# A linear-attention and expert-attention kernel: one drawn-up order for all instructions, fixed buffers, and scores on row halves

## The chip, the cores and the metric

The kernel runs on one core of one Trainium2 chip. A core has TensorE (PE) for matrix products, with PSUM banks as its output; VectorE (DVE), ScalarE (ACT) and GpSimd (POOL) for elementwise work; SyncE (SP) and the other engines' queues issue the transfers (DMAs) between HBM and SBUF. The metric is device time in microseconds (us). Before the change the median of three runs is 376.76 us (375.64 to 377.31).

## The reference, cut to what matters

A gated linear attention makes x, and a small mixture of four attention experts with a top-2 gate works on x. All of it is float32.

```python
# q, k, v, alpha: (4, 8, 768, 48); alpha in 0.8 to 1
for t in range(S):
    state = alpha[:, :, t, :, None] * state + einsum('bhd,bhe->bhde', k[:, :, t], v[:, :, t])
    y[:, :, t] = einsum('bhd,bhde->bhe', q[:, :, t], state)
x = y.transpose(0, 2, 1, 3).reshape(4, 768, 384)
logits = x @ w_gate                              # (384, 4): the two largest of 4, softmax over them
for e in range(4):
    q, k, v = x @ wq[e], x @ wk[e], x @ wv[e]    # (384, 64) each
    scores = where(causal, -1e9, scale * (q @ k.T))
    a = softmax(scores)
    ye = a @ v @ wo[e]                           # (64, 384)
    out += (e is one of the two) * gate_weight * ye
```

## The kernel before, in words

**Tiles.** The 768 positions of each of four batches are cut into six chunks of 128, so there are 24 chunks. Three chunks are one unit of the expert attention: eight units, u = 0 to 7, of 384 positions. Heads come in pairs, one on partitions 0 to 47 and one on 64 to 111.

**Linear attention, per chunk.** Three loads bring decay factors (al, line 85), queries with keys (qk, line 94) and values (v, line 100). DVE scans the decay factors backwards (line 187, into r) and forwards (line 197, into c), takes reciprocals (line 190), and multiplies keys by r (line 199) and queries by c (line 200). PE makes the products pa of keys and queries, two row halves of 48 rows, 8 matmuls of 128 columns into two PSUM banks, named pa. Each of the two banks is masked: the first by a DVE product (line 219); the second for chunks 0 to 2 also by DVE, and for later chunks by an ACT copy (line 221) and a POOL select (line 222). Four transposes (pt) and eight small matmuls (pu) update the state: DVE adds (line 256), POOL multiplies (line 257), or DVE alone (line 254) in a batch's first chunk. PE forms py, x of the chunk; ACT copies it to a rounded high half xh (line 283), and DVE subtracts to get a low half xl (line 284). ACT sums the squares of al (line 204) for a check on its range.

**Expert attention, per unit.** The front of a unit is four projections pj (9 matmuls of 384 columns each: high times high, high times low, low times high), three value projections pv, and the gate on DVE. The back is twelve score tiles (two pairs of experts, two experts, three groups of 128 rows), their softmax and the rest. Before, a score uses fp32r operands: queries and keys as high and low halves, stacked over 128 partitions, so that two matmuls over 128 rows make one tile. The high halves are ACT copies (lines 411, 434), the low halves are DVE subtractions (lines 412, 435, 430, 431), and transfers on SP from SBUF to SBUF (lines 418 and 438) put the halves on the partitions where they are wanted. DVE adds the causal mask, writes the tile and finds the row minimum of its negative (line 503); ACT takes the exponential (line 506), DVE the reciprocals of the sums (lines 514, 515), POOL multiplies with these and the gate (line 520). PE transposes (line 537, tr), ACT copies (line 548), PE multiplies by the values (yv) and, with a high and a low half again (lines 568, 569), by wo (po). ACT copies to ot (line 580), SP stores (line 583).

**What sets the order.** The function `head()` (lines 306 to 346) lists the work of the first three chunks by hand, in `tc.manual_schedule()`. Behind it `mix()` (line 633) draws from streams: a unit's back, the next unit's front, and the chunks of the unit after that (`gla()`, line 367). Each stream has a weight (`MIX_BACK`, `MIX_FRONT`, `MIX_GLA`), and the stream that has had the least matmul cost by its weight goes next. Tiles come from pools whose buffers rotate: eight PSUM banks for all products, 3 buffers for al and v, 4 for qk, 7 for score tiles a. `gla()` issues its loads on ACT's queue, the head on SP's. Matmuls on zeros (`warm()`, 56 in all) stand between the head's steps. At the very end (lines 657 to 664) DVE counts the chunks whose squares are in range, a matmul with ones sums the count (line 660, pk), a cast stores it (line 662), and a branch on the value picks a slow repetition of everything if it falls short.

## Time and profile before

| | before |
|---|---|
| median of 3 runs | 376.76 us (375.64 to 377.31) |
| the profiled execution | 377.36 us |
| its span in the trace | 375.6 us |
| mean granted clock of PE | 0.967 |
| PE busy | 339.1 us, 90% of the span |
| DVE busy | 256.6 us, 68% |
| ACT busy | 215.5 us, 57% |
| POOL busy | 117.6 us, 31% |
| HBM read and written | 24.44 and 4.72 MB, 78 GB/s over the span |

The span is the time from the first to the last event in the trace of the profiled execution; its own time is 1.76 us longer. An engine's busy time is the time in which it executes something; register, branch, semaphore and issuing instructions are not counted. The granted clock is a share of TensorE's full clock, 2.4 GHz. A high busy share over the whole run says little about one stage of it, so the rows further down also cut the run into stretches.

### The profile page before, as it was taken

The numbers are of one execution on the slowest core, as the hardware profiler recorded it, in microseconds if no ns is written. First come the engines' busy times: TensorE is split into PE (matmuls) and PEld (weight loads), VectorE is DVE, ScalarE is ACT, GpSimd is POOL, SyncE is SP. The second block draws the span as 40 slices with busy tenths as digits, with TensorE's granted clock in tenths as the row PEclk, the third lists the DMA queues.
The fourth block names the chain that finished last, engine by engine and source line by source line (L and its number), as shares of the span: only waits on it lengthen the run. The fifth ranks groups of instructions, "written<-read, shape, count | busy, mean of one in ns | idle before, by whom it ended". The sixth has DMA issues, their size and how long they took to land.

```text
span 375.6 us, 9749 instructions
## 1 busy us (share of the span) xinstructions
PE 339.1 (90%) x3654; PEld 283.9 (76%) x3654; DVE 256.6 (68%) x729; ACT 215.5 (57%) x540; POOL 117.6 (31%) x192
## 2 busy tenths in 40 slices
PE   7879829889976999899899999999999999999993
PEld 5568717678955977687779888787889977988772
DVE  5999998687777979367857889175538641576610
ACT  1246555644434978275546896375548853868740
POOL 2040139402123750034403751043305620425500
PEclk9899965999998999999999999999999999999997
DMA  7764671368477334564376525463264005541101
GB/s 241 282 205 120 126 179 26 103 206 217 126 179 186 121 101 115 156 171 115 98 172 176 145 92 142 128 157 88 66 162 119 4 7 156 144 111 50 42 23 52
DMA packets 23400, 47.97 MB, mean 128 GB/s; under 512 B 3536, under 2 KB 10416, under 8 KB 23344
## 3 DMA queue, kind: packets, MB, share of 16 engines
q1 hardware_dynamic: 15744, 29.39, 29.3%
q10 hardware_dynamic: 7600, 17.87, 17.0%
q8 instruction: 31, 0.51, 0.6%
q14 instruction: 25, 0.20, 0.2%
HBM read 24.44 MB, written 4.72 MB: 78 GB/s over the span
## 4 chain that ended last, share of the span: by engine, by line
PE 62%; DVE 15%; DMA 9%; ACT 7%; issue 4%; POOL 2%; ACTq 0%; DVEq 0%; POOLq 0%; SPq 0%
PE pj L72 10%; PE yv L72 10%; PE sc L72 8%; PE tr L537 8%; PE py L72 7%; PE po L72 7%; PE pv L72 5%; DMA al<-in_al_dram 5%; PE pa L72 3%; DVE al L187 3%; DMA qk<-in_qk_dram 2%; DVE al L197 2%; ACT al L204 2%; DMA q<-tq 2%; PE pu L72 2%
## 5 line engine op out<-in xcount | busy, mean ns | idle before, releaser
L520 POOL TENSOR_SCALAR a<-a,sc,gw 128x128 f32<-128x128 f32 (+5 forms) x96 | 76.2, 804 | 84.2 <-DVE sc L515 52.1
L506 ACT ACTIVATE a<-a,mx 128x512 f32<-128x512 f32 (+5 forms) x96 | 63.7, 665 | 33.7 <-DVE mx L503 33.1
L72 PE MATMUL sc<-k,q 128*128 128x384 f32 (+3 forms) x256 | 59.2, 348 | 6.5 <-DVE xl L284 3.2
L503 DVE CUSTOM_DVE_ANT_0 a<-sc,cm 128x384 f32<-128x384 f32 (+3 forms) x96 | 49.3, 528 | 17.4 <-PE sc L72 15.1
L537 PE MATMUL tr<-ident,a 128*128 128x128 f32 x336 | 50.5, 280 | 7.6 <-POOL a L520 7.6
L548 ACT ACTIVATE at<-tr 128x512 f32<-128x512 f32 (+3 forms) x124 | 49.6, 460 | 4.3 <-PE tr L537 3.9
L72 PEld LDWEIGHTS sc<-k,q 128*128 128x128 f32 x256 | 42.2, 196 | 11.4 <-DVE xl L284 3.5
L72 PE MATMUL yv<-at,vg 128*64 128x384 f32 (+2 forms) x324 | 47.0, 394 | 2.9 <-ACT at L548 2.9
L537 PEld LDWEIGHTS tr<-ident,a 128*128 128x128 f32 x336 | 39.2, 143 | 13.3 <-POOL a L520 9.9
L72 PEld LDWEIGHTS yv<-at,vg 128*64 128x64 f32 x324 | 24.5, 136 | 23.4 <-issue 12.7
L72 PE MATMUL py<-ms,v 128*32 128x128 f32 x768 | 36.7, 285 | 3.1 <-DVE ms L219 1.6
L187 DVE TENSOR_TENSOR_SCAN al<-al,d1r 112x516 f32<-112x516 f32 (+1 forms) x25 | 29.6, 1184 | 13.9 <-DMA al<-in_al_dram 13.9
L72 PE MATMUL pj<-xl,wqk_h 128*128 128x384 f32 x96 | 33.2, 346 | 2.2 <-DVE xl L284 2.2
L72 PE MATMUL pj<-xh,wqk_h 128*128 128x384 f32 x96 | 34.5, 361 | 0.8 <-ACT xh L283 0.6
L257 POOL TENSOR_TENSOR S<-st,ev 48x192 f32<-48x192 f32 x32 | 16.9, 528 | 56.2 <-DVE st L256 55.2
L191 POOL COPY ev<-al 112x4 f32<-112x4 f32 (+1 forms) x25 | 6.4, 256 | 87.5 <-DVE S L254 51.0
L72 PE MATMUL pj<-xh,wqk_l 128*128 128x384 f32 x96 | 33.0, 344 | 0.0
L204 ACT ACTIVATE al<-al 112x1033 f32<-112x1033 f32 x23 | 24.6, 1069 | 14.1 <-POOL ev L191 5.4
L197 DVE TENSOR_TENSOR_SCAN al<-al,d1c 112x516 f32<-112x516 f32 (+1 forms) x25 | 30.6, 1223 | 0.5
L72 PE MATMUL pa<-qk 48*128 48x128 f32 x384 | 28.2, 285 | 2.4 <-issue 1.5
L72 PEld LDWEIGHTS py<-ms,v 128*32 128x32 f32 x768 | 23.0, 113 | 9.2 <-DVE ms L219 3.0
L72 PEld LDWEIGHTS pa<-qk 48*128 48x128 f32 x384 | 23.4, 187 | 4.8 <-issue 2.0
(98 smaller groups left out, 645.3 us busy)
## 6 DMA issues: line engine op xcount, KB each, us to landing
q<-tq SPq DMA_DIRECT2D x64, 192.0 KB, 3.6
qk<-in_qk_dram ACTq DMA_DIRECT2D x18, 448.0 KB, 4.6
k<-tk SPq DMA_DIRECT2D x56, 96.0 KB, 3.1
v<-in_v_dram ACTq DMA_DIRECT2D x19, 256.0 KB, 3.9
out_dram<-ot SPq DMA_DIRECT2D x24, 192.0 KB, 1.9
al<-in_al_dram ACTq DMA_DIRECT2D x18, 226.2 KB, 2.9
qk<-in_qk_dram SPq DMA_DIRECT2D x5, 448.0 KB, 5.9
v<-in_v_dram SPq DMA_DIRECT2D x5, 256.0 KB, 6.1
```

Source lines behind the costliest of these rows:

```text
L72: return PE.matmul(out, lhsT, rhs, **kw)
L187: V.tensor_tensor_scan(backwards(al[0:P, AW + c0 - 1:AW + c1 - 1]), backwards(al[0:P, c0:c1]), d1r[0:P, sl].rearrange("p a w -> p (a w)"), ...
L191: G.tensor_copy(gl["ev", n][0:P, sl], r[:, :, 0])
L197: V.tensor_tensor_scan(c.rearrange("p a w -> p (a w)"), c.rearrange("p a w -> p (a w)"), d1[0:P, sl].rearrange("p a w -> p (a w)"), 0.0, O ...
L204: A.activation(al, al, AF.Square, accum_out=acc[0:P, n:n + 1])
L257: G.tensor_tensor(Ln[rows, :, cols], st[rows], e, OP.mult)
L503: V.tensor_tensor_reduce(a[:, c0:c1], pp[:, :w], cm[:, m0:m0 + w], -1.0, mx[:, 0:1] if x else BIG, OP.add, OP.min, accum_out=mx[:, x:x + 1])
L506: A.activation(a[:, 0:n], a[:, 0:n], AF.Exp, bias=nm, scale=-1.0, accum_out=sm)
L520: G.tensor_scalar(a[:, 0:n], a[:, 0:n], cf[:, x:x + 1], mo["w", u][:, i, eg:eg + 1], op0=OP.mult, op1=OP.mult)
L537: PE.transpose(pt[:, 128 * (j - j0):128 * (j - j0) + 128], a[:, 128 * j:128 * j + 128], ident)
L548: A.activation(dst, src, AF.Copy)
```

## The change

**A plan in place of pools and streams.** A class `Plan` takes each piece of work as a record: engine, the time for which it occupies the engine, the time until its result is there, what it reads and writes, and a function that issues it. `schedule()` walks through time: of the records on each engine whose inputs are there and whose buffers are free it takes the one that can start first (within `LOOK` = 0.05 us the earlier record in the source), and allots one of a fixed number of buffers. The durations are numbers in the source, as `vec`, `act`, `pol` and constants for PE. `emit()` issues all records in that order in `tc.manual_schedule()`, and puts matmuls on zeros into PE's gaps of over 0.45 us before 45 us of the plan's time, 88 in all. The streams and `mix()` still set the order of the records in the source.

**Buffers.** Seven PSUM banks for products, and one for the matmuls on zeros; 4 buffers for al, qk, values and ev, 8 score tiles, 4 for at, 2 for ms.

**Scores.** Queries and keys are ACT copies in f32, one tile per pair of experts, with one expert on partitions 0 to 63 and the other on 64 to 127. A score is one f32 matmul over 64 rows for each expert, the two side by side on row halves. The low halves of queries and keys and the transfers from SBUF to SBUF are gone. Score matmuls go from 256 to 128. Scores are made per pair of experts, `AHEAD` is 3 pairs in place of 5 tiles.

**Other edits.** All loads go through SP. The second mask goes to ACT and POOL for all chunks (`MS_DVE = 0`). The check at the end stands behind the last po.

**How the orders differ.** On DVE, at the head, the instructions up to the one that subtracts chunk 2's low half (xl) in the order before. In it al and qk are decay factors and queries with keys, d1c holds reciprocals, ms is a mask's result, S and st are states, and a scan is named SCALAR_TENSOR_TENSOR on al:

```order
L187 SCALAR_TENSOR_TENSOR al<-al,d1r 112x516
L190 RECIPROCAL d1c_80<-al 112x4
L199 TENSOR_TENSOR qk<-qk,al 112x4x128
L219 TENSOR_TENSOR ms<-pa_343,mask 128x512
L219 TENSOR_TENSOR ms<-pa_344,mask 128x512
L197 SCALAR_TENSOR_TENSOR al<-al,d1c_80 112x516
L172 SCALAR_TENSOR_TENSOR wqk_l<-wqk,wqk_h 128x3x256
L176 TENSOR_TENSOR wqk_l<-wqk,wqk_h 128x3x256
L200 TENSOR_TENSOR qk<-qk,al 112x4x128
L284 TENSOR_TENSOR xl<-py,xh 128x3x128
```

The same place on DVE in the new order, where g_63 to g_69 are the seven PSUM banks, at_137 holds the raw weights and al_73 and qk_77 belong to chunk 3:

```order
L454 TENSOR_TENSOR ms_90<-g_67,mask 128x512
L393 SCALAR_TENSOR_TENSOR al_73<-al_73,d1r 112x516
L397 RECIPROCAL d1c_87<-al_73 112x4
L508 TENSOR_TENSOR st_93<-g_63,S_95 48x192
L338 SCALAR_TENSOR_TENSOR wqk_l<-at_137,wqk_h 128x3x256
L342 TENSOR_TENSOR wqk_l<-at_137,wqk_h 128x3x256
L548 TENSOR_TENSOR xl_98<-g_69,xh_96 128x3x128
L508 TENSOR_TENSOR st_93<-g_63,S_95 48x192
L416 SCALAR_TENSOR_TENSOR al_73<-al_73,d1c_87 112x516
L420 TENSOR_TENSOR qk_77<-qk_77,al_73 112x4x128
```

Chunk 3's second scan and its products moved from ahead of chunk 2's low half to behind it, and one of chunk 2's two masks left DVE.

On PE, scores of the second unit in the order before, with transposes (tr) of other tiles between them; k_579 and k_580 are the keys of the two experts of a pair, x2 stands for the high and the low queries:

```order
L72 MATMUL sc<-k_579,q 128x512 x2
L72 MATMUL sc<-k_579,q 128x256 x2
L537 MATMUL tr<-ident,a 128x128 x4
L72 MATMUL sc<-k_580,q 128x512 x2
L537 MATMUL tr<-ident,a 128x128 x5
```

The corresponding place on PE in the new order, where k_105 and q_103 hold two experts each and line 698 is the transposes:

```order
L642 MATMUL g_66<-k_105,q_103 128x512
L642 MATMUL g_68<-k_105,q_103 128x512
L698 MATMUL g_65<-ident,a_133 128x128 x4
L698 MATMUL g_63<-ident,a_134 128x128 x4
L642 MATMUL g_69<-k_105,q_103 128x256
L642 MATMUL g_67<-k_105,q_103 128x256
L642 MATMUL g_64<-k_105,q_103 128x384
L642 MATMUL g_65<-k_105,q_103 128x384
```

Two consecutive matmuls of one tile became two consecutive matmuls of two tiles, one for each expert, which hold two banks at once.

On SP, the queue in the order before, from the last loads of the head on; tq and tk are the halves that transfers from SBUF to SBUF put in place, ot is an output tile:

```order
L100 DMA v<-in_v_dram 128x512
L94 DMA qk<-in_qk_dram 112x1024
L85 DMA al<-in_al_dram 112x517
L418 DMA q<-tq 64x768 x8
L583 DMA out_dram<-ot 128x384 x3
L418 DMA q<-tq 64x768 x4
L438 DMA k_448<-tk 64x384 x2
L438 DMA k_449<-tk 64x384 x2
```

SP's queue in the new order, at the first stores; al_72, qk_77 and vt_81 are buffers of decay factors, queries with keys, and values:

```order
L311 DMA qk_77<-in_qk_dram 112x1024
L316 DMA vt_81<-in_v_dram 128x512
L307 DMA al_72<-in_al_dram 112x517
L767 DMA out_dram<-ot_145 128x384
L767 DMA out_dram<-ot_146 128x384
L307 DMA al_73<-in_al_dram 112x517
L767 DMA out_dram<-ot_145 128x384
L311 DMA qk_74<-in_qk_dram 112x1024
L316 DMA vt_78<-in_v_dram 128x512
```

The loads of all later chunks came into SP's queue, between stores, and the transfers of queries and keys left it.

The core of the diff:

```diff
-AB = 7
-XB = 2
...
+AHEAD = 3
+HOP = 0.1
...
+ISSUE = 3.0
+SEM = 0.07
+DMA_FIXED = 1.5
+DMA_RATE = 220.0
+LOOK = 0.05
+WARM_UNTIL = 45.0
+WARM_GAP = 0.45
+WARM_MM = 0.11
+GB = 7
+MS_DVE = 0
+class Plan:
...
+    def schedule(self, timed=True):
+        ops, pools = self.ops, self.pools
+        slot_of, done = {}, [None] * len(ops)
+        free = {p: [(0.0, x) for x in range(len(t))] for p, t in pools.items()}
...
+            if timed:
+                for e, lst in ready.items():
+                    c = [(est(i), i) for i in lst]
+                    c = [x for x in c if x[0] is not None]
+                    if not c:
+                        continue
+                    lo = min(x[0] for x in c)
+                    t, i = min((x for x in c if x[0] <= lo + LOOK), key=lambda x: x[1])
+                    if best is None or t < best[0]:
+                        best = (t, i)
...
+            o["start"] = t
+            at[e] = t + o["occ"]
+            end = t + o["lat"]
+            if o["dma"]:
+                dma_at = max(t + DMA_FIXED, dma_at) + o["dma"] / DMA_RATE / 1e3
+                end = dma_at
+            o["end"] = end
...
+            for j in succ[i]:
+                same = ops[j]["eng"] == e and not o["dma"]
+                rt[j] = max(rt[j], t + o["occ"] if same else end + SEM)
...
+    def emit(self, warm=None):
+        pe = ISSUE
+        for i in self.order:
+            o = self.ops[i]
+            if warm is not None and o["eng"] == "PE":
+                gap = o["start"] - pe
+                if o["start"] < WARM_UNTIL and gap > WARM_GAP:
+                    warm(int(gap / WARM_MM * 0.8))
+                pe = o["start"] + o["occ"]
+            o["fn"](self.tile)
...
+    pools = {
+        "g": [ps.tile([128, 512], F32, name=f"g_{x}") for x in range(GB)],
+        "al": slots("al", 4, [128, 2 * AW - 1]),
+        "qk": slots("qk", 4, [128, 4, 2 * C]),
+        "vt": slots("vt", 4, [128, 4, 128]),
+        "ev": slots("ev", 4, [128, 4]),
+        "d1c": slots("d1c", 2, [128, 4, CW]),
+        "kt": slots("kt", 2, [128, 4, P]),
+        "ms": slots("ms", 2, [128, 2, 4, C]),
...
+        "q": slots("q", 4, [128, W3]),
+        "k": slots("k", 3, [128, S]),
+        "vg": slots("vg", 3, [128, 3, 260]),
+        "gt": slots("gt", 1, [128, 2, 3, NE, NE]),
...
+        "a": slots("a", 8, [128, S]),
+        "at": slots("at", 4, [128, W3 * NT - W3]),
...
+        def load_al(n, p0=0, np=4):
+            c0 = CW * p0 + (p0 > 0)
+            c1 = CW * (p0 + np) + 1
+            op("S", 0.06, 0, lambda T: SY.dma_start(T(("al", n))[0:P, c0:c1], al_d[n, :, c0:c1]),
+               w=[(("al", n), ("c", p)) for p in range(p0, p0 + np)], dma=P * 4 * (c1 - c0))
+
+        def load_q(n, p0=0, np=4):
+            op("S", 0.06, 0, lambda T: SY.dma_start(T(("qk", n))[0:P, p0:p0 + np], qk_d[n, :, p0:p0 + np]),
+               w=[(("qk", n), p) for p in range(p0, p0 + np)], dma=P * 1024 * np)
...
+                if s == 0 or n < MS_DVE:
+                    op("V", 0.61, 0.69, f0, r=whole(("pa", n, s), ("mask",)), w=[(("ms", n), s)])
+                else:
+                    op("A", *act(512), f1, r=whole(("pa", n, s)), w=[(("ms", n), s)])
+                    op("G", 0.64, 0.7, f2, w=[(("ms", n), s)])
...
+            if which == 0:
+                op("A", *act(W3), lambda T: A.activation(T(("q", u, pair)), T(("pj", u, pair, 0))[:, :W3], AF.Copy),
+                   r=whole(("pj", u, pair, 0)), w=whole(("q", u, pair)))
             else:
...
+                op("A", *act(W3), lambda T: A.activation(T(("k", b, pair))[:, W3 * hf:W3 * hf + W3],
+                                                         T(("pj", u, pair, 1))[:, :W3], AF.Copy),
+                   r=whole(("pj", u, pair, 1)), w=[(("k", b, pair), hf)])
...
+                def f(T, c0=c0, c1=c1, w=w, sk=sk):
+                    q, k = T(("q", u, pair)), T(("k", b, pair))
+                    for e in (0, 1):
+                        r = slice(64 * e, 64 * e + 64)
+                        PE.matmul(T(sk[e])[:, :w], q[r, ts], k[r, c0:c1], start=True, stop=True,
+                                  tile_position=(64 * e, 0))
+                occ = 2 * (0.008 + w / 1200) + 0.1
...
+        def chunk(n):
+            loads(n + 2)
+            prep_r(n)
+            if n % NC:
+                gla_u(n - 1)
+            prep_c(n)
+            yield
+            gla_a(n)
+            if n % NC != NC - 1:
+                gla_t(n)
+            check(n)
+            yield
+            gla_y(n)
+            yield
...
-            if n + 2 < NG:
-                load_v(n + 2, A)
-            if n + 3 < NG:
-                load_al(n + 3, 0, 4, A)
-                load_q(n + 3, 0, 4, A)
-            gla_y(n)
-            gla_u(n)
...
-        if which == 0:
-            tq = work.tile([128, 2, W3], F32R, name="tq", bufs=1)
-            A.activation(tq[:, 0], pj[:, :W3], AF.Copy)
-            V.tensor_tensor(tq[:, 1], pj[:, :W3], tq[:, 0].bitcast(F32), OP.subtract)
...
-                q = work.tile([128, 2, W3], F32R, name="q", bufs=QB)
-                src = tq[64 * e:64 * e + 64].bitcast(F32)
-                for h in (0, 1):
-                    SY.dma_start(q[64 * h:64 * h + 64].bitcast(F32), src)
...
-            pp = gp("sc")
-            w = c1 - c0
-            mm(pp[:, :w], qh[:, ts], ks[:, c0:c1], max(w, 256) / 2.4, start=True, stop=False)
-            mm(pp[:, :w], ql[:, ts], ks[:, c0:c1], max(w, 256) / 2.4, start=False, stop=True)
-            m0 = 640 - w if c1 == n else 0
-            V.tensor_tensor_reduce(a[:, c0:c1], pp[:, :w], cm[:, m0:m0 + w], -1.0, mx[:, 0:1] if x else BIG,
-                                   OP.add, OP.min, accum_out=mx[:, x:x + 1])
```

## Rows read from the trace of the kernel before

**Rows 1.** The page's first part: busy us, share of the span and instructions of each engine over the whole run.

```profile
PE 339.1 (90%) x3654; PEld 283.9 (76%) x3654; DVE 256.6 (68%) x729; ACT 215.5 (57%) x540; POOL 117.6 (31%) x192
```

**Rows 2.** The run cut into four stretches. Columns: the stretch and its length in us, then the busy us (and instructions) of PE, PE's weight loads, DVE, ACT and POOL, then PE's granted clock, the DMA share and GB/s.

```profile
0.00:29.50 29.50, 22.95 (x297) 16.97 (x297) 24.92 (x43) 9.68 (x16) 7.25 (x25) 0.94 0.71 232
29.50:119.00 89.50, 71.87 (x877) 60.66 (x878) 73.42 (x165) 43.56 (x107) 26.21 (x43) 0.92 0.60 151
119.00:369.40 250.40, 244.32 (x2482) 206.29 (x2480) 158.26 (x523) 161.78 (x418) 84.11 (x124) 0.99 0.41 109
369.40:375.60 6.20, 0.00 (x0) 0.00 (x0) 0.00 (x0) 0.49 (x1) 0.00 (x0) 0.64 0.16 49
```

**Rows 3.** Pieces of the chain that ended last, over the whole run. Columns: start in us, duration in us, what it was, with the number of matmuls in the piece. Line 72 is the helper that issues all matmuls; the names tell them apart.

```profile
83.63 1.01 PE py L72 x32
...
99.41 1.68 PE py L72 x56
101.58 1.09 PE pa L72 x16
...
128.10 1.08 PE pv L72 x9
...
138.85 3.38 PE yv L72 x24
142.81 1.60 PE pj L72 x9
...
192.64 3.38 PE po L72 x18
...
281.77 3.07 PE sc L72 x18
...
307.31 2.84 PE tr L537 x26
```

**Rows 4.** The score matmuls of the whole run, grouped by shape. Columns: line, engine, operation, output and inputs, shapes, count, then busy us and mean ns of one (pipelined, so one overlaps the next), then the idle us before them and what ended it.

```profile
L72 PE MATMUL sc<-k,q 128*128 128x512 f32 x64 | 21.6, 418 | 2.9 <-DVE mx L503 2.3 <-DVE xl L284 0.6
L72 PE MATMUL sc<-k,q 128*128 128x256 f32 x96 | 21.2, 303 | 2.5 <-DVE xl L284 2.5
L72 PE MATMUL sc<-k,q 128*128 128x384 f32 x64 | 18.9, 375 | 0.0
...
L72 PE MATMUL sc<-k,q 128*128 128x128 f32 x32 | 6.5, 286 | 1.1 <-PE sc L72 0.6 <-issue 0.5
```

**Rows 5.** Three further pieces of the chain, just ahead of the third unit's first projection (the last row).

```profile
103.27 7.59 DMA q<-tq
...
112.67 3.42 DMA al<-in_al_dram
...
119.07 2.88 PE pj L72 x9
```

**Rows 6.** DVE's instructions in order of time, ahead of the first projection that runs through. Columns: start in us, duration in us, engine, line, operation, output and inputs, shapes.

```profile
23.48 0.72 DVE L199 TENSOR_TENSOR qk<-qk,al 112x512 f32<-112x512 f32 x1
24.24 1.29 DVE L219 TENSOR_TENSOR ms<-pa,mask 128x512 f32<-128x512 f32 x2
25.44 1.22 DVE L197 TENSOR_TENSOR_SCAN al<-al,d1c 112x516 f32<-112x516 f32 x1
...
28.30 0.69 DVE L200 TENSOR_TENSOR qk<-qk,al 112x512 f32<-112x512 f32 x1
28.90 0.55 DVE L284 TENSOR_TENSOR xl<-py,xh 128x384 fp32r<-128x384 f32 x1
```

**Rows 7.** DVE's groups between 29.5 and 119 us, by shape (columns as in rows 4), and, as the last row, the same stretch for the tile pj alone: busy us of PE, PE's weight loads, DVE and ACT on it, then clock, DMA share and GB/s. Its DVE column holds all low halves of queries and keys.

```profile
L187 DVE TENSOR_TENSOR_SCAN al<-al,d1r 112x516 f32<-112x516 f32 x12 | 14.7, 1227 | 5.6 <-DMA al<-in_al_dram 5.6
...
L199 DVE TENSOR_TENSOR qk<-qk,al 112x512 f32<-112x512 f32 x9 | 6.6, 735 | 2.2 <-DMA qk<-in_qk_dram 2.1
...
L219 DVE TENSOR_TENSOR ms<-pa,mask 128x512 f32<-128x512 f32 x8 | 5.5, 688 | 0.2
L256 DVE TENSOR_TENSOR st<-pu,S 48x192 f32<-48x192 f32 x12 | 4.2, 349 | 0.2
L284 DVE TENSOR_TENSOR xl<-py,xh 128x384 fp32r<-128x384 f32 x7 | 3.8, 544 | 0.8 <-ACT xh L283 0.7
L412 DVE TENSOR_TENSOR tq<-pj,tq 128x384 fp32r<-128x384 f32 x5 | 2.8, 552 | 3.3 <-ACT tq L411 3.3
...
29.50:119.00 89.50, 15.58 (x80) 14.05 (x81) 6.00 (x11) 5.24 (x11) 0.92 0.60 151
```

**Rows 8.** The second mask's two instructions over the whole run, on POOL and ACT (columns as in rows 4).

```profile
L222 POOL TENSOR_SCALAR_AFFINE_SELECT ms<-ms 128x512 f32<-128x512 f32 x21 | 14.7, 699 | 11.1 <-ACT ms L221 10.9
L221 ACT ACTIVATE ms<-pa 128x512 f32<-128x512 f32 x21 | 12.5, 593 | 12.6 <-PE pa L72 9.9 <-PE pt L230 1.7 <-POOL ev L191 0.6
```

**Rows 9.** An issue of a load on SP's queue and one on ACT's, from the order of time. Columns: start in us, duration in us, queue, line, what is moved.

```profile
2.20 0.43 SPq L94 DMA_DIRECT2D qk<-in_qk_dram  x1
...
31.46 0.32 ACTq L85 DMA_DIRECT2D al<-in_al_dram  x1
```

**Rows 10.** The end of the run, on PE and DVE in order of time: the check's matmul, the last output matmul, and the cast that stores the check's count.

```profile
368.28 0.19 PE L660 MATMUL pk<-ones,okm 112*1 112x1 f32 x2
...
368.90 0.44 PE L72 MATMUL po<-wo_h,yl 128*128 128x384 f32 x1
...
368.51 0.15 DVE L662 CAST cnt<-pk 1x1 int32<-1x1 f32 x1 [2.44 <-PE pk L660]
```

More of the change, by code (lines that the diff above doesn't have):

```diff
@@ L26 @@
 NT = S // 128
+W3 = 384
 P = 112
@@ new lines, in tile_gla_moe, with cst @@
+    kinds = {p: p for p in pools}
+    kinds.update(pa="g", pt="g", pu="g", py="g", pj="g", pv="g", sc="g", tr="g", yv="g", po="g")
+    def cst(shape, name, dt=F32):
+        return consts.tile(shape, dt, name=name)
+    d1r = cst([128, 4, CW], "d1r")
+    ident = cst([128, 128], "ident")
+    mask = cst([128, C], "mask")
+    acc = cst([128, NG], "acc")
+    cm = cst([128, 640], "cm")
+    lm = cst([128, NE, NE], "lm")
+    ones = cst([128, 1], "ones")
+    wqk_h = cst([128, 3, 512], "wqk_h", F32R)
@@ L336, in head @@
+        wload(1)
+        constants3()
+        run(chunk(2))
         split_hi(0)
@@ L629, in chain @@
+        split_lo(3)
+        half = lambda h: gla(h) if h < NU else None
+        b, g = chain(front(0), back(0)), half(1)
+        mix((b, MIX_BACK0), (g, MIX_GLA0), until=g)
+        for u in range(NU - 2):
+            mix((b, MIX_BACK[u]), (front(u + 1), MIX_FRONT[u]), (half(u + 2), MIX_GLA))
+            b = back(u + 1)
+        f = front(NU - 1)
+        mix((b, MIX_BACK6), (f, MIX_FRONT7), until=f)
+        mix((b, MIX_TAIL6), (back(NU - 1), MIX_TAIL7))
     def chain(*gs):
@@ L631, in chain @@
             yield from x
-    def mix(*streams, until=None):
-        live = [[g, w, 0.0] for g, w in streams if g is not None]
-        while live and (until is None or any(x[0] is until for x in live)):
-            x = min(live, key=lambda z: z[2] / z[1])
-            c0 = cost[0]
-            if next(x[0], 1) == 1:
-                live.remove(x)
-            x[2] += cost[0] - c0 + HOP
-    half = lambda h: gla(h) if h < NU else None
-    with tc.manual_schedule():
-        head()
-    body()
@@ L657, in tile_gla_moe, with warm @@
+    pl = Plan(pools, kinds)
+    build(pl, True)
+    pl.schedule()
+    pw = ps.tile([128, 512], F32, name="pw")
+    def warm(k):
+        for _ in range(k):
+            PE.matmul(pw[:, 0:256], zb[:, 0:128], zb, start=True, stop=True)
+    with tc.manual_schedule():
+        pl.emit(warm)
+    okm = cst([128, NG + 1], "okm")
     V.tensor_scalar(okm[0:P, 1:], acc[0:P], SAFE, None, op0=OP.is_le)
     V.tensor_reduce(okm[0:P, 0:1], okm[0:P, 1:], axis=AX.X, op=OP.add)
-    pk = gp("pk")
+    pk = pools["g"][0]
@@ L666, in tile_gla_moe @@
         yd = dram_pool.tile([B * H, S, D], F32, name="yd")
-        sel = work.tile([128, 32], F32, tag="cb", bufs=1, name="sel")
+        sel = pools["kt"][0][:, 0, 0:32]
         G.memset(sel, 0.0)
```

1193 lines of the change are left out of this document (658 added, 535 removed).

## The prediction

> **What bounds the kernel now.** I read the page's busy shares first, then the run cut into stretches, then the chain of waits, then DVE's instructions in one stretch. PE is busy 90% of the span and DVE 68% [rows 1]. An average hides where the time goes, so the second view cuts the run at three instants: the first projection that runs through (29.5 us), the first projection of the third group of three chunks (119.07), the end of the last output matmul (369.4) [rows 2]. In the long stretch from 119 on PE is busy 244.3 of 250.4 us: this part is bound by PE, and only 6.1 us are idle. In the head PE waits for the first chunks. Between 29.5 and 119 PE is busy 71.9 of 89.5 us at a granted clock of 0.92, and DVE 73.4 of 89.5: here DVE feeds PE, and what holds up DVE shows in the chain. The longest piece there is a transfer of queries from SBUF to SBUF, 7.59 us at 103.27, then a load of decay factors, 3.42 us, and then the third group's projection can start [rows 5].
>
> The sum is made on the profiled execution: 377.36 us, of which 375.6 is the span, so 1.76 lies around it. It stands 0.6 us above the median of the runs, 376.76.
>
> **The change part by part.**
>
> *Head.* DVE decides when the first projection starts: its last input is the low half of chunk 2's x, at 28.90 [rows 6]. In the new order four things no longer stand ahead of that instruction: the second scan of chunk 3 (1.22 us at 25.44), chunk 3's two products (0.72 at 23.48 and 28.30 to 28.90, 1.3), and the second of the two masks for each of chunks 0 to 2 (a pair takes 1.29 at 24.24, so 0.6 each, 1.8). 28.90 - 1.2 - 1.3 - 1.8 = 24.6, and the projection follows half a microsecond later: 25. The second mask now costs an ACT copy of 0.59 and a POOL select of 0.70 [rows 8], in sum the 1.29 that the pair took on DVE, so PE gets it no later unless ACT is busy with other work. I keep 24.5 to 27.
>
> All loads now go through SP. There an issue takes 0.43 us, on ACT 0.32 [rows 9]. Chunk 0's four pieces used two queues; now they follow each other, so the last is issued three issues behind the first instead of one, some 0.9 us later. DVE reads it last in chunk 0, behind all four scans of that chunk; if this cover is gone, the head is 0.9 us later, inside the range above.
>
> *Second stretch, up to the third group's first projection.* What PE has to do there, by its place in the new order: 8 projections at 1.60, 6 value projections at 1.08, 6 py (5 at 1.68, one without a state at 1.01), 7 pa at 1.09, 24 transposes at 0.109, 2 short yv, 3 po at 1.13, 7 score pairs and the small pt and pu, 54 us by the steps of the chain [rows 3]. DVE needs longer. Its 73.4 us before, less what goes or is not in the new order up to that point: 11 low halves of queries and keys, 6.0 us; two first scans of 12, 2.5; two masks of 8, 1.4; five state additions of 12, 1.7; two low halves of x of 7, 1.1 [rows 2, 7]. 73.4 - 12.7 = 60.7, and 60 with two score pieces fewer. So DVE stays the bound. It was idle for 16.1 of the 89.5 us, a share of 0.82: 5.6 before first scans waiting for decay loads, 2.1 before products waiting for queries and keys, 3.3 before the low halves waiting for ACT's copy [rows 7]. The last go with the low halves. The loads get four buffers for three, and an engine that has no other work. That leaves 5 us of waits; I take 4, so 60 + 4 = 64: the stretch ends at 25 + 64 = 89, where it ended at 119. Ends: no wait (85) and the old share (60 / 0.82 = 73, 98).
>
> *Third stretch.* The same work for PE as before: 250.4 us, 6.1 of them idle. I take half the idle time away: 247.4.
>
> *Scores.* 256 matmuls over 128 rows become 128 over 64 rows in full f32, two heads side by side. Before: 18 in 3.07 [rows 3], 0.17 each, 44 us. Half of the old counts by width [rows 4] leave 32 x 512 + 32 x 384 + 48 x 256 + 16 x 128 = 43,008 columns. No row shows this shape. The nearest is pa, two row halves of 48 rows in f32: 1024 columns in 1.09 us, 1.064 ns a column, which gives 45.8 us; yv, f32 with two column halves, takes 3.38 us for 3840 columns, 0.88 ns, which gives 37.9. I take 43.5, near pa since that is the same row split: -0.5 against 44, with -6 and +2 as ends. The weight loads go from 256 to 128 and lie beside matmuls in both.
>
> One thing speaks against the change here. A pa group of 1024 columns takes 0.19 us more than yv's rate would give (1.09 - 0.90) [rows 3], and the new order has 41 separate groups of scores: 41 x 0.19 = 7.8 us over 37.9, or 45.7. The Trainium skill, TensorEngine Tiling (Array Packing), Key Properties, says that changing the tiling mode drains the engine; before, the scores ran in the same full mode as the transposes beside them. By that rule the sum is 2 us longer than mine; without any drain it is 6 us shorter. The pa row agrees with a drain of at most 0.2 us in and out together.
>
> *DVE, ACT, POOL and PSUM later on.* The low halves of q and k, 552 ns each on DVE [rows 7], and the transfers behind them all go; ACT's copies of q and k stay. Behind 119 DVE was busy 158.3 of 250.4 us [rows 2], so this gives nothing there: PE covers it. PSUM banks go from eight to seven. A score pair holds two until DVE has read them, pa two; three are left. I put nothing, and 0 to 3 us if PE must wait for a bank.
>
> *End.* After the last po (ended at 369.34) came 6.3 us. The check that follows was laid among the last matmuls; its result stood at 368.66 [rows 10], 6.9 us before the end. Now its matmul stands behind the last po, so its result comes some 0.35 us after po, as its matmul and cast take 0.34 now: if the branch needs 6.9 us from there, 7.2. I take 7; ends 6.3 and 7.3.
>
> Sum: 25 + 64 + 247.4 - 0.5 + 7 = 342.9, and 1.76 around it: 344.7; I say 344.
>
> **Rivals.**
>
> *DVE keeps waiting.* The order on each engine is fixed: if one instruction is late, all behind it are. Then the share stays 0.82 in the second stretch (73 us) and the third stays as it was: 25 + 73 + 250.4 + 7 + 1.8 = 357. For it: 7.2 of the 16.1 us idle were waits for neither decay loads nor ACT's copies. Against it: the long single waits there are transfers [rows 5].
>
> *PE never waits.* DVE without a wait (85), 2 us idle in the third stretch (246.3), scores at yv's rate (-6), end 6.3: 85 + 246.3 - 6 + 6.3 + 1.8 = 333. For it: PE already reached 244.3 of 250.4. Against it: DVE's chain of scans, products, pa and masks is served in one queue.
>
> *Row halves do not overlap.* One pass of 128 columns takes 0.109 us (a transpose, 26 in 2.84 [rows 3]), and an f32 matmul has two: 1.70 ns a column, 73 us for the scores, 29.6 more than I took: 374. Against it: pa would then need 1.74 us a group and takes 1.09.
>
> *Slower: loads that stand behind others.* One in-order queue on SP now holds all loads of decay factors, queries with keys, and values, and the 24 stores. A load waits for a free buffer, a store for an output tile, and all behind them wait too; before, ACT issued most loads and SP the stores. A chunk whose decay factors come late stops its scan and DVE's queue with it, as the 3.42 us in the chain at 112.67 did [rows 5]. 20 chunks after the first four at 3 us each make 60: 404. It decides from (376.8 - 344) / 20 = 1.6 us a chunk on. Against it: in the new order a decay load stands up to four chunks ahead of its scan.
>
> **How the numbers follow.** My forecast 0.52 (own range 335 to 353); DVE keeps waiting 0.22 (357); PE never waits 0.15 (333); no overlap 0.05 (374); loads 0.06 (404). The range for 8 in 10 reaches from 329, below the second rival by the half of a bank's or drain's doubt, to 360, above the first. All but the last are faster; 0.5% (1.9 us) is what a measurement of this kernel can tell from no change, and half of the overlap case with its own doubt lies near that bound: 0.92 faster, 0.02 the same, 0.06 slower.
>
> **What would show it.** The first projection near 25 us; DVE busy over 90% from there to the third group's first projection, which starts near 89; PE over 97% busy behind it; no DMA piece over 2 us in the chain after the head; a score pair with 512 columns at 0.9 to 1.1 us from start to start (1.7 would mean no overlap). It is wrong if DVE waits for ACT or PE over 8 us in sum in the second stretch, if the chain has decay loads again, or if PE's idle time in the third exceeds 8 us.

## The result and the profile after

The changed kernel takes 363.39 us (362.71 to 364.09, median of 4 runs) beside 377.03 us for the kernel before on the same chip: a ratio of 0.964, with a 95% interval of 0.961 to 0.968. It is faster, as forecast, but 19 us slower than the 344 of the forecast and above the range, which ended at 360. The profiled execution has a span of 361.0 us; before it was 375.6.

The page's first part after the change [rows 1], and the run cut at three instants (columns as in [rows 2]): the start of the first projection of the first unit, the start of the first projection of the third unit, the end of the last output matmul.

```profile
PE 337.9 (94%) x3686; PEld 264.9 (73%) x3686; DVE 244.3 (68%) x692; ACT 216.3 (60%) x543; POOL 124.7 (35%) x190
```

```profile
0.00:26.80 26.80, 23.18 (x341) 18.33 (x341) 21.07 (x36) 11.07 (x19) 9.26 (x27) 1.00 0.93 244
26.80:91.60 64.80, 59.75 (x756) 48.92 (x753) 63.03 (x141) 39.45 (x100) 24.03 (x34) 1.00 0.49 137
91.60:354.30 262.70, 254.97 (x2594) 197.68 (x2594) 160.09 (x516) 165.28 (x426) 91.37 (x130) 0.99 0.18 54
354.30:361.00 6.70, 0.01 (x1) 0.00 (x0) 0.15 (x1) 0.47 (x1) 0.00 (x0) 0.70 0.14 44
```

Three of the four stretches are within 2 us of the forecast: 26.8 (25), 64.8 (64), 6.7 (7). The third has 262.7, where 246.9 was forecast: 15.8 of the 18.1 us by which the span exceeds its forecast of 342.9. (The forecast's own instant for the end of the head comes 1 us later, at 27.75; see *Head* below.)

The reason stands in the trace of before. These are PE's projections of the third unit there, in order of time:

```profile
103.53 0.33 PE L72 MATMUL pj<-xh,wqk_h 128*128 128x384 f32 x1
105.86 0.45 PE L72 MATMUL pj<-xl,wqk_h 128*128 128x384 f32 x1 [2.00 <-DVE xl L284]
...
118.86 0.53 PE L72 MATMUL pj<-xh,wqk_h 128*128 128x384 f32 x1
```

The third unit's first projection begins at 103.5, not at 119. What the chain shows at 119.07 [rows 5] is its second. Cut at the same place as after the change, the kernel before reads:

```profile
0.00:27.90 27.90, 21.71 (x292) 16.25 (x292) 23.32 (x40) 8.08 (x14) 7.25 (x25) 0.94 0.75 245
27.90:103.50 75.60, 63.05 (x762) 53.44 (x763) 64.05 (x145) 40.87 (x100) 22.42 (x34) 0.91 0.54 138
103.50:369.40 265.90, 254.38 (x2601) 214.22 (x2599) 169.24 (x546) 166.07 (x427) 87.91 (x133) 0.99 0.43 114
```

Now the stretches can be compared: head -1.1, second -10.8, third -3.2, end +0.5, in sum -14.6, which is the whole difference of the spans. PE's busy time hardly moved (339.1 to 337.9). Its idle time did: 6.2 + 12.6 + 11.5 + 6.2 = 36.5 before, 3.6 + 5.1 + 7.7 + 6.7 = 23.1 after. The busy time holds the matmuls on zeros, 9.9 us before and 12.9 after. In the second stretch PE was also 3.3 us less busy with about as many matmuls, at a granted clock of 1.00 for 0.91.

### The profile page after: what moved, and what is told of

The parts are those of the page before. It is cut to its first block, busy times and chain, and to the rows that moved or that the text cites. A ratio compares the mean times of both kernels' runs of the same rounds, so it can differ in the third digit from the quotient of the medians.

```text
span 361.0 us, 9454 instructions
## 1 busy us (share of the span) xinstructions
PE 337.9 (94%) x3686; PEld 264.9 (73%) x3686; DVE 244.3 (68%) x692; ACT 216.3 (60%) x543; POOL 124.7 (35%) x190
## 4 chain that ended last, share of the span: by engine, by line
PE 54%; DVE 30%; issue 5%; ACT 4%; DMA 3%; POOL 1%; ACTq 0%; DVEq 0%; POOLq 0%
PE g L735 9%; PE g L698 9%; PE g L567 8%; PE g L642 8%; DVE al L416 6%; PE g L535 6%; PE g L760 5%; DVE al L393 5%; PE g L585 4%; DVE a L652 4%; PE g L445 3%; DVE qk L424 2%; DMA al<-in_al_dram 2%; DVE qk L420 2%; DVE ms L454 2%
## 5 line engine op out<-in xcount | busy, mean ns | idle before, releaser
L680 POOL TENSOR_SCALAR a<-a,cf,gw 128x128 f32<-128x128 f32 (+5 forms) x96 | 78.4, 827 | 130.3 <-DVE cf L674 85.8
L661 ACT ACTIVATE a<-a,mx 128x128 f32<-128x128 f32 (+5 forms) x96 | 63.2, 660 | 18.2 <-DVE mx L652 16.2
L652 DVE CUSTOM_DVE_ANT_0 a<-g,cm 128x384 f32<-128x384 f32 (+3 forms) x96 | 47.8, 530 | 35.0 <-PE g L642 30.7
L712 ACT ACTIVATE at<-g 128x512 f32<-128x512 f32 (+3 forms) x124 | 49.5, 456 | 7.8 <-PE g L698 7.7
L642 PE MATMUL g<-k,q 64*128 64x256 f32 (+3 forms) x256 | 49.7, 478 | 2.1 <-ACT ot L765 2.0
L698 PE MATMUL g<-ident,a 128*128 128x128 f32 x336 | 49.2, 283 | 1.8 <-POOL a L680 1.5
L698 PEld LDWEIGHTS g<-ident,a 128*128 128x128 f32 x336 | 38.1, 143 | 13.5 <-POOL a L680 5.1
L735 PE MATMUL g<-at,vg 128*64 128x384 f32 (+2 forms) x324 | 41.4, 393 | 1.4 <-ACT at L712 1.4
L535 PE MATMUL g<-ms,vt 128*32 128x128 f32 x768 | 36.0, 277 | 6.4 <-DVE ms L454 4.7
L567 PE MATMUL g<-xh,wqk_h 128*128 128x384 f32 x96 | 35.2, 367 | 0.5 <-DVE xl L548 0.5
L535 PEld LDWEIGHTS g<-ms,vt 128*32 128x32 f32 x768 | 23.4, 109 | 15.8 <-DVE ms L454 5.9
L642 PEld LDWEIGHTS g<-k,q 64*128 64x128 f32 x256 | 22.5, 185 | 13.8 <-issue 4.6
L511 POOL TENSOR_TENSOR S<-st,ev 48x192 f32<-48x192 f32 x32 | 21.2, 663 | 28.0 <-DVE st L508 26.8
## 6 DMA issues: line engine op xcount, KB each, us to landing
at<-in_wo_dram SPq DMA_DIRECT2D x1, 384.0 KB, 11.5
```

The source lines that it names most:

```text
L535: PE.matmul(py[32 * j:32 * j + 32, k], l, r, start=(i == 0), stop=(i == len(parts) - 1), tile_position=(0, 32 * j))
L567: PE.matmul(pj[:, :W3], w[:, kt, cs], x[:, kt, :], start=(i == 0), stop=(i == 8))
L642: PE.matmul(T(sk[e])[:, :w], q[r, ts], k[r, c0:c1], start=True, stop=True, tile_position=(64 * e, 0))
L652: V.tensor_tensor_reduce(T(ak[e])[:, c0:c1], T(sk[e])[:, :w], cm[:, m0:m0 + w], -1.0, mx[:, 0:1] if x else BIG, OP.add, OP.min, accum_out= ...
L661: A.activation(a[:, 0:n], a[:, 0:n], AF.Exp, bias=T(mk)[:, e, len(pieces) - 1:len(pieces)], scale=-1.0, accum_out=T(("sm", u))[:, ix:ix + 1])
L680: G.tensor_scalar(a[:, 0:n], a[:, 0:n], T(ck_)[:, e:e + 1], T(("gw", u))[:, i, eg:eg + 1], op0=OP.mult, op1=OP.mult)
```

## The experiments

Kernels whose label begins with a_ are the changed kernel with an edit, those with b_ the kernel before. They ran on several chips, on which the kernel before took 376.0 to 378.2 us (medians); a ratio is to the kernel before on the same chip.

### Row halves and order, each without the other

a_hilo puts the scores back to high and low halves, with DVE's low halves and the transfers on SP, which also holds the loads there; the order is drawn up anew. The core of its edit:

```diff
-                        PE.matmul(T(sk[e])[:, :w], q[r, ts], k[r, c0:c1], start=True, stop=True,
-                                  tile_position=(64 * e, 0))
+                        for h in (0, 1):
+                            PE.matmul(T(sk[e])[:, :w], q[:, h, ts], k[:, c0:c1], start=(h == 0), stop=(h == 1))
```

> The changed kernel with the scores as before: high and low halves in fp32r stacked over 128 rows, low halves on DVE, transfers from SBUF to SBUF on SP; the order is drawn up anew by the list scheduler (3 buffers of at for 4, to make room). Theory A, the row halves gain: scores cost PE some 50 us for 46, DVE has 32 more instructions of 0.55, 6 us of them in the second stretch, and scores wait for transfers: 370 to 378. Theory B, drains at the change of tiling eat the gain of the row halves: 358 to 365. Either way the gap from a transpose to a score falls from 0.20 us to about 0.03.

387.18 us (384.06 to 390.25), ratio to before 1.020 (1.012 to 1.027): slower even than theory A has it. The time from the start of a transpose to the start of a score behind it fell to 0.029 us. The waits of PE show the largest cost (engine and line, what it waited for: us, times, longest), here and in a_hilo2, where the plan knows how long a transfer takes (0.55 us of issue, and a `lag` of 3.0 us for transfers from SBUF to SBUF):

```profile
PE g L663 <- DMA q<-tq: 16.1, 5, 4.4
```

```profile
PE g L664 <- DMA q<-tq: 12.4, 4, 4.5
```

```diff
-                end = dma_at
+                end = dma_at + o["lag"]
```

> The changed kernel with high and low halves as in the run before (387 us), but the plan now gives each transfer from SBUF to SBUF the 0.55 us of issue and some 3 us to landing that the traces show, so that the scheduler puts other work into that time. Theory A, what the row halves bring is that nothing waits for transfers: PE's wait for them falls from 16.1 us to under 4, and the time to 367 to 374. Theory B, the halves cost PE or DVE itself the time: it stays at 380 to 387.

378.55 us (375.19 to 380.32), no faster than before, and between the two theories. PE still waits 12.4 us for transfers, so only a part of theory A held. a_tight keeps the row halves, with about as few buffers as a_hilo had, counted in pairs of experts (q 2 for 4, k 2 for 3, at 3 for 4):

> The changed kernel with f32 row-half scores, but with no more buffers than the run with high and low halves had: 2 tiles of queries for 4, 2 of keys for 3, 3 of at for 4. There the time was 379 to 387 us. Theory A, the transfers and their waits made that: here 362 to 366. Theory B, the missing buffers made it: 372 to 380.

363.61 us: these buffers are not the cause. What is left is the transfers, with the single tiles (tq, tk) that they are sent from, and the queue that they share with the loads. The other way round, b_f32 puts row halves into the old order, and b_pair only the order by pairs that they need, with the halves kept; both make scores 2 pairs ahead. The core of b_f32's edit:

```diff
-            mm(pp[:, :w], qh[:, ts], ks[:, c0:c1], max(w, 256) / 2.4, start=True, stop=False)
-            mm(pp[:, :w], ql[:, ts], ks[:, c0:c1], max(w, 256) / 2.4, start=False, stop=True)
+            for e in (0, 1):
+                r = slice(64 * e, 64 * e + 64)
+                mm(pp[e][:, :w], q[r, ts], k[r, c0:c1], max(w, 256) / 1.2, start=True, stop=True,
+                   tile_position=(64 * e, 0))
```

> The kernel before with one part of the change: f32 scores on row halves, both experts of a pair side by side, no low halves and no transfers of queries and keys (8 score tiles for 7, 2 pairs ahead for 5 tiles). If the row halves make most of the gain: 361 to 367. If the drawn-up order makes most of it: 372 to 378. If each makes half: 368 to 372.

385.44 us (385.06 to 386.40), ratio 1.020 (1.016 to 1.024): slower, which none of the three cases had.

> The kernel before with high and low halves as they were, but with the scores of the two experts of a pair next to each other, normalized and transposed pair by pair, as the run with row halves that took 385 us (7 score tiles, 8 there). Theory A, this order costs, not the row halves: 383 to 389. Theory B, the changes of tiling cost: 375 to 379.

377.82 us (375.82 to 379.03), ratio 1.000 (0.997 to 1.004). So the order by pairs costs nothing, and the row halves, with the low halves and transfers gone, cost these 8 us. The last two stretches of b_pair, then of b_f32 (columns as in [rows 2]):

```profile
28.00:103.20 75.20, 63.40 (x764) 54.24 (x765) 64.56 (x144) 39.99 (x100) 20.32 (x34) 0.91 0.52 136
103.20:370.00 266.80, 253.50 (x2599) 214.81 (x2598) 169.61 (x546) 164.65 (x427) 91.03 (x133) 1.00 0.42 115
```

```profile
27.80:103.10 75.30, 64.19 (x765) 51.40 (x765) 61.29 (x137) 40.25 (x98) 20.13 (x34) 0.89 0.37 106
103.10:377.20 274.10, 261.79 (x2600) 201.14 (x2598) 154.72 (x520) 164.64 (x426) 92.78 (x133) 1.00 0.17 54
```

In the third stretch PE is 8.3 us busier with as many records (an f32 matmul has two), and no idler. DVE is 15 us less busy, which gains nothing. Where PE's time goes shows between groups, in order of time, in b_pair and then in b_f32:

```profile
285.38 1.04 PE L538 MATMUL tr<-ident,a 128*128 128x128 f32 x8
286.17 1.18 PE L72 MATMUL sc<-k,q 128*128 128x512 f32 x4
```

```profile
288.96 1.03 PE L518 MATMUL tr<-ident,a 128*128 128x128 f32 x8
289.93 1.13 PE L72 MATMUL sc<-k,q 64*128 64x512 f32 x4
```

After eight transposes the scores start 0.79 us from the first transpose in full tiles, and 0.97 us on row halves. Over all places where a score follows a transpose, 18 in each, the median from the last transpose's start to the first score's is 0.029 and 0.203 us. By the trace some 35 of the 41 groups of scores lie in the third stretch; 8.3 / 35 = 0.24 us a group, net of what the scores inside a group gain.

b_f32b is b_f32 with `AHEAD` 3 for 2 and 10 score tiles for 8.

> The kernel before with f32 scores on row halves, as in the run that took 385 us, with 3 pairs ahead and 10 score tiles instead of 2 and 8. If the smaller distance cost the time there: 374 to 379. If the changes of tiling on PE did (PE's work without zeros 337 us there for 329.5 before): 383 to 387.

399.42 us (398.56 to 400.14): both expectations missed. PE is busy 272.3 us in its third stretch, 10.5 more than in b_f32. 6.2 of these are in yv (300 records in 50.2 us, 44.0 in b_f32). PE waits 11.7 us there for ACT's copies ahead of yv (5.1 in b_f32), up to 3.3 at a time, and the granted clock is 0.98 for 1.00; from 130 to 140 us, around the longest of these waits, it is 0.83. So a part is the lower clock after waits. Why ACT's copies come later with more distance stays open.

### What bounds each stretch

a_po2 leaves out a third of the output projection, the high half of y times the low half of wo.

> The changed kernel with the output projection's third product left out (high half of y times low half of wo): 48 matmuls of some 0.176 us less, 8.4 us, of which 42 lie behind the third group's first projection. Theory A, PE's work bounds everything from there on: the time falls by 7 to 9 us, to 354.5 to 356.5. Theory B, waits for other engines bound it: it falls by less than 4.

358.11 us (355.56 to 358.97), 5.3 less, between the two theories; in the profiled execution, the fastest of the four, 7.2 less. Its second and third stretch:

```profile
26.80:91.60 64.80, 58.69 (x750) 47.89 (x747) 63.02 (x141) 39.35 (x100) 24.02 (x34) 1.00 0.50 137
91.60:347.60 256.00, 248.12 (x2552) 190.36 (x2552) 159.89 (x516) 164.54 (x426) 91.36 (x130) 1.00 0.18 55
```

42 matmuls fewer make the third stretch 6.7 us shorter and PE 6.9 us less busy: in this execution PE's own work bounds it. By the medians, up to 2 us of that does not come out. The six that lie in the second give nothing there. What DVE means in that stretch, a_ms24 (`MS_DVE = 24`) and a_kpool ask:

> The changed kernel with the second mask on DVE for all chunks, 24 more DVE products of 0.69 us, 3 of them in the head and some 7 in the second stretch, and as many ACT copies and POOL selects less. Theory A, DVE bounds the head and the second stretch and PE the rest: the first projection 1.8 us later, the third group's first 5 to 7 us later, nothing behind it: 368 to 371. Theory B, DVE bounds the third stretch too: 375 to 380. Theory C, the scheduler finds room: 362 to 365.

360.06 us (359.47 to 361.52): faster than the changed kernel, which only theory C came near. The third unit starts at 91.0, and DVE is busy 61.6 of 63.1 us in the second stretch. Theory A had the masks make that stretch 5 to 7 us longer, and they did not; the order was drawn up anew. a_kpool moves the product of keys to POOL:

```diff
-                V.tensor_tensor(t, t, suffixes(T, n)[:, sl, 1:CW], OP.mult)
+                G.tensor_tensor(t, t, suffixes(T, n)[:, sl, 1:CW], OP.mult)
```

> The changed kernel with the product of keys and backward scans on POOL instead of DVE, 24 instructions of 0.7 us off DVE, some 9 of them in the second stretch and 3 in the head, at perhaps 1.2 us each on POOL (an estimate from POOL's 0.53 for 192 elements and 0.70 for its 512-element select). Theory A, DVE's busy time bounds the second stretch: the third group's first projection 3 to 6 us earlier, and 358 to 361 us. Theory B, its chain from load to product bounds it, and the longer POOL instruction makes it later: 364 to 370.

364.33 us, and the third unit starts at 95.5, four later. DVE's product of queries over the whole run, before (the changed kernel) and with POOL's product beside it (columns as in [rows 4]):

```profile
L424 DVE TENSOR_TENSOR qk<-qk,al 112x512 f32<-112x512 f32 x23 | 16.3, 709 | 0.0
```

```profile
L420 POOL TENSOR_TENSOR qk<-qk,al 112x512 f32<-112x512 f32 x23 | 31.2, 1358 | 35.7 <-DMA qk<-in_qk_dram 28.1 <-DVE al L393 3.6 <-PE g L698 3.3
...
L424 DVE TENSOR_TENSOR qk<-qk,al 112x512 f32<-112x512 f32 x23 | 23.3, 1013 | 4.2 <-DMA qk<-in_qk_dram 4.0
```

POOL takes 1.36 us for what took DVE 0.75, and DVE's own product goes from 0.71 to 1.01 us on average: it takes 0.68 us where nothing of POOL's runs beside it, and up to 1.69 where POOL's product began first. That agrees with the Trainium skill, SBUF — State Buffer (the section "SBUF: two separate sides"), by which a DVE operation with two SBUF inputs and a GpSimd operation that reads SBUF shut each other out. The work was taken off DVE and came back as waiting; whether DVE's busy time alone bounds the stretch is not settled by it.

### The queue of the loads

b_spq moves the later loads of the old kernel to SP, a_actq those of the new kernel to ACT.

> The kernel before with one edit, the loads of the later chunks issued on SP's queue, behind its transfers and stores, in place of ACT's. If the loads' place on ACT's queue made DVE wait for decay factors (5.6 us in the second stretch): 370 to 374. If not: 376 to 379. If loads then stand behind transfers and stores, the slower rival of the prediction: over 382.

391.64 us, ratio 1.040 (1.033 to 1.046). DVE's waits for loads over the whole run, in b_spq and then in the kernel before:

```profile
DVE qk L199 <- DMA qk<-in_qk_dram: 12.0, 6, 4.7
...
DVE al L187 <- DMA al<-in_al_dram: 3.6, 4, 2.1
```

```profile
DVE al L187 <- DMA al<-in_al_dram: 13.9, 10, 3.8
...
DVE qk L199 <- DMA qk<-in_qk_dram: 4.4, 3, 2.3
```

> The changed kernel with the loads of chunks 3 to 23 on ACT's queue, 63 issues of some 0.33 us, as before the change; the plan counts 0.35 us of ACT for each. Theory A, one queue for loads was no part of the gain, and the four buffers are: 361 to 366. Theory B, loads behind ACT's work come late again, decay loads stand in the chain: 368 to 375.

362.41 us (361.55 to 362.75). So one queue costs the old kernel 14 us, where 120 transfers from SBUF to SBUF and the stores share it with the loads. The way that the slower rival of the forecast gave is not shown: DVE waits 15.6 us for loads in sum, and 18.3 before. In the new kernel the transfers are gone, and the choice of queue is worth no more than the 1 us between the medians; whether that is so because the transfers are gone, or because of the fourth buffer or the order, was not tried. a_actq's first projection came late, at 31.7, while its third stretch was 3 us shorter.

### Order, zeros and combinations

a_src issues the records in the order of the source (`pl.schedule(timed=False)`).

> The changed kernel, but with all records issued in the order of the source instead of the order of the list scheduler; buffers, row-half scores and loads on SP stay (the matmuls on zeros in gaps of the plan become 201 from 88). Theory A, the order makes the gain: PE and DVE wait as they did before, 370 to 385 us. Theory B, buffers, loads and scores make it and the scheduler adds little: 360 to 366.

530.74 us. Neither theory was near. PE waits 57.4 us for DVE's products of queries, 15 times, ahead of pa: in the order of the source pa stands close behind the products that it needs. PE waits for these 0.9 us in the kernel before, so this is no measure of the old order.

a_nowarm (`WARM_UNTIL = 0.0`):

> The changed kernel without matmuls on zeros. Before the change the granted clock was at half for some 20 us between 10 and 130 us, after it for 3.4 us. Theory A, the clock is a part of the gain and the zeros hold it up: the granted clock falls below full in the head and the time rises to 366 to 372. Theory B, PE waits for DVE there anyway and the clock hides nothing: 362 to 365.

362.25 us (361.37 to 363.91): theory B. Without zeros the granted clock is 1.00 in the head and in the second stretch. Before the change it was 0.91 in the second stretch, where PE was idle for 12.6 us: from 48 to 56 us PE was busy for 1.7 us, and from 52 to 64 us the clock was at its lower level (0.50 to 0.51).

a_ah4 (`AHEAD = 4`, 10 score tiles), a_best1 (a_ms24 and a_nowarm), a_comb (a_kpool and a_ah4), a_c1 (a_ms24 and a_ah4), a_c2 (a_ah4 and ACT's queue from chunk 6 on):

> The changed kernel with scores made 4 pairs ahead of their transposes instead of 3, with 10 score tiles instead of 8. PE was idle 7.7 us behind the third group's first projection, and short waits stand inside groups of transposes. If waits for POOL's normalization make these: 358 to 361. If PE's own work bounds: 362 to 365.

361.31 us, between its two cases.

> The changed kernel with the second mask on DVE for all chunks and no matmuls on zeros, the two that by themselves gave 360.1 and 362.3 us for 363.4. If both gains are real and add up: 358.5 to 359.5. If they are the luck of one order drawn up anew: 359.5 to 363.

361.43 us (360.45 to 362.17): the second case, the two do not add up.

> The products of keys on POOL and 4 pairs ahead with 10 score tiles together. If each takes its idle time away: 356 to 359. If PE's work bounds and each is only another order: 360 to 363.

367.99 us: slower than either alone, and outside both cases.

> The changed kernel with the second mask on DVE for all chunks (alone 360.1) and 4 pairs ahead with 10 score tiles (alone 361.3). If the gains add: 357.5 to 359. If each is only another fall of the order: 359.5 to 363.

359.36 us (357.76 to 361.55), ratio to before 0.955 (0.950 to 0.959): with a_c2 the fastest here that leaves no work out. Gains of 3.3 and 2.1 would make 358.0, which the scatter of its runs does not rule out.

> The changed kernel with 4 pairs ahead and 10 score tiles, and the loads from chunk 6 on on ACT's queue (loads from chunk 3 on gave 362.4, with the first projection 5 us late and the third stretch 3 us shorter). If the late start was the issues' place in the head: 357 to 360. If not: 361 to 364.

359.69 us (358.85 to 361.06), and the first projection at 26.8 again: the late start of a_actq was the place of the issues in the head. Each edit of the changed kernel lets the scheduler draw up another order, but for a_nowarm and a_po2, which leave matmuls out of the same order, and a_src. Those that keep row halves and all of the work lie between 359.4 and 364.3 us, a_comb aside; below that spread, a cause can't be read from one of them.

## Why the prediction was right or wrong

**The step that failed** is "the stretch ends at 25 + 64 = 89, where it ended at 119", and with it "Third stretch. The same work for PE as before: 250.4 us". The forecast ended its second stretch at the first projection of the third unit, and the row of before was its second projection. Between the two lay 15.5 us of the old run, 10.1 of them PE work (254.38 - 244.32) that the new order has to do as well, in its third stretch. By the cut at 103.5 the same method gives 25 + 64 + 260.2 (265.9 less half of 11.5 idle) - 0.5 + 7 + 1.8 = 357.5, where the profiled execution took 362.7. A warning stood in the prediction itself: DVE's sum had work taken out as "not in the new order up to that point", and nothing put it back behind.

**Head.** The forecast's 25 stands for the first projection that runs through, 29.5 in the old run. After the change that is the matmul at 27.75, not the one at 26.8:

```profile
26.80 0.42 PE L567 MATMUL g<-xh,wqk_h 128*128 128x384 f32 x1
27.75 0.44 PE L567 MATMUL g<-xl,wqk_h 128*128 128x384 f32 x1 [0.53 <-DVE xl L548]
```

So the head missed by 2.8 us and left its range, which ended at 27. The four things left the front of DVE's queue, but the low half of chunk 2 was done at 27.69 and not at 24.6:

```profile
22.29 0.56 DVE L548 TENSOR_TENSOR xl<-g,xh 128x384 fp32r<-128x384 f32 x1 [1.65 <-ACT xh L544]
...
23.36 1.67 DVE L393 TENSOR_TENSOR_SCAN al<-al,d1r 112x516 f32<-112x516 f32 x1
...
27.15 0.54 DVE L548 TENSOR_TENSOR xl<-g,xh 128x384 fp32r<-128x384 f32 x1
```

DVE waited 1.65 us for an ACT copy, which the chain shows behind ACT's sum of squares: the case "unless ACT is busy with other work". One scan took 1.67 us for 1.25. These make 2.1 of the 3.1 us; the rest is not accounted for.

**Second stretch.** 64 forecast, 63.8 measured from 27.75 on (64.8 from 26.8), and DVE is busy 97% of it, as said. The sum is in part luck: 60 of work and 4 of waiting were forecast, and 62.1 of work and 1.7 without came. Of the rival "DVE keeps waiting" nothing came. The groups that answer to [rows 7], from 26.8 to the third unit's first projection:

```profile
L393 DVE TENSOR_TENSOR_SCAN al<-al,d1r 112x516 f32<-112x516 f32 x10 | 12.2, 1222 | 0.0
L420 DVE TENSOR_TENSOR qk<-qk,al 112x512 f32<-112x512 f32 x9 | 6.6, 737 | 0.0
...
L454 DVE TENSOR_TENSOR ms<-g,mask 128x512 f32<-128x512 f32 x6 | 4.1, 686 | 0.2
L548 DVE TENSOR_TENSOR xl<-g,xh 128x384 fp32r<-128x384 f32 x7 | 3.8, 543 | 0.2 <-ACT xh L544 0.2
L508 DVE TENSOR_TENSOR st<-g,S 48x192 f32<-48x192 f32 x7 | 2.5, 351 | 0.1
```

The first scans, masks and state additions are as many as forecast (10, 6, 7); of low halves of x there are seven, one of them chunk 2's at 27.15, and the forecast had five. No scan waits for its load there. By the right cut the stretch gained 10.8 us (75.6 to 64.8), not the 25.5 of the forecast (89.5 to 64).

**Scores.** Forecast 43.5 us for 44. Taken from each start to the next start, less idle time, the scores take PE 46.2 us after and 50.5 before. The 44 was too low: 0.17 each was read from 18 in a row at full clock, and over all 256 matmuls, in 70 groups, it is 0.197. The shape's own rate was better than the best end of the range: inside a group a pair of 512 columns takes two passes of 0.43 us, 0.86 in all (0.84 ns a column, where yv has 0.88). Between other work such a pair takes 1.06. What it costs is the change of tiling. The 0.19 us a group read from pa is borne out in size by b_pair and b_f32 (0.24 a group, 8.3 us of PE in the third stretch). That is the direction of the rule in the Trainium skill, TensorEngine Tiling (Array Packing), Key Properties, by which a change of tiling mode drains the engine. The forecast set these costs against a base that was too low for the old kernel, and so had -0.5. In the new order PE is busy 335.3 us in a_hilo2 and 337.9 in the changed kernel, so the row halves cost it 2.6 there; they gain by the waits for transfers that go (12.4 us in a_hilo2). The groups that answer to [rows 4]:

```profile
L642 PE MATMUL g<-k,q 64*128 64x512 f32 x64 | 18.8, 625 | 2.0 <-ACT ot L765 2.0
...
L642 PE MATMUL g<-k,q 64*128 64x256 f32 x96 | 17.2, 414 | 0.1
...
L642 PE MATMUL g<-k,q 64*128 64x384 f32 x64 | 14.2, 510 | 0.0
...
L642 PE MATMUL g<-k,q 64*128 64x128 f32 x32 | 4.1, 310 | 0.0
```

One record of 512 columns is longer than before (625 ns for 418), but two run at once, so the busy time of all is smaller. Busy times by shape hide what the groups cost at their ends. The weight loads of the scores did not go from 256 to 128: the trace has 256 records before and after, 42.2 us of PEld before and 22.5 after.

**End.** 7 was forecast for the time after the last po; it ended at 354.20 (353.86 + 0.34), 6.8 us before the span's end. The check's cast now stands behind it:

```profile
353.86 0.34 PE L760 MATMUL g<-wo_h,yl 128*128 128x384 f32 x1
354.12 0.19 PE L953 MATMUL g<-ones,okm 112*1 112x1 f32 x2
```

```profile
354.35 0.15 DVE L955 CAST cnt<-g 1x1 int32<-1x1 f32 x1 [0.76 <-PE g L953]
```

**Signs.** PE over 97% busy behind 91.6: 255.0 of 262.7 is 97.1%, and its idle time there, 7.7 us, is just under the 8 that were named as a sign of being wrong. "No DMA piece over 2 us in the chain after the head" was wrong, and decay loads in the chain, another such sign, came. They can weigh little, as PE's whole idle time in that stretch is 7.7 us:

```profile
155.60 2.54 DMA al<-in_al_dram
...
168.50 2.96 DMA al<-in_al_dram
...
178.77 4.63 DMA out_dram<-ot
```

**Where the gain came from.** Neither part of the change gains alone. Old order with halves 377.0, old order with row halves 385.4, new order with halves 378.6 at best, new order with row halves 363.4. In the old order the row halves cost PE 8 us; in the new order, the halves make PE wait 12 to 16 us for transfers. In the kernel before PE waits for no transfer, and in b_pair for this:

```profile
PE sc L72 <- DMA q<-tq: 2.2, 2, 1.5
```

But the new order with halves differs from the old one in a third thing: the loads share SP's queue with the transfers, as in b_spq, which lost 14 us by it. The new order with halves and the loads on ACT's queue was not run. So how much of its 15 us over the changed kernel is the order, and how much the queue, stays open.

## What to carry to other kernels

When two orders of the same work are compared by stretches, mark each boundary by the same instruction in both, by counting it out in the trace, and let what leaves one stretch come back in another; the busy sum of the bounding engine over the whole run is the check. Where that engine is at 90% and keeps its work and its clock, the gain is at most its idle time (here 36.5 us, of which 13.4 went). Scores on row halves cost PE more at their changes of tiling than they saved it here; they paid only where waits for transfers went with the halves.

## What was not expected of the hardware

Going from full tiles to row halves and back costs PE some 0.24 us a group of scores, net of what the scores gain (0.17 of it between the last transpose and the first score), although the two matmuls of a pair run side by side and share a pass of 0.43 us for 512 columns. With a two-input product on POOL in the stream, a two-input DVE product took 43% longer on average (709 to 1013 ns). In the changed kernel the matmuls on zeros did nothing for the granted clock: it is 1.00 in the first two stretches with and without them.
